# Eight more dummy matmuls in the head of an attention and expert-mixing kernel

## Chip, cores, metric

One core of one Trainium2 chip. The metric is the device time of one launch in microseconds (us). The profiler's span of an execution is 1.7 to 2.4 us shorter than its time; both are used below, and it is said which. Faster or slower needs 2%.

## The reference

Attention with decay (RetNet) over 8 batches, 8 heads, 576 positions and 64 values a head; its output goes through four experts, each two matmuls with a ReLU, weighted by normalised probabilities. Shortened:

```python
def _attn_ref(q, k, v):
    scores = scale * np.matmul(q, k.transpose(0, 1, 3, 2))
    # Dmat[h, i, j] = gamma[h] ** (i - j) for i >= j, else 0
    return np.matmul(scores * Dmat, v)

def _moe_ref(x, domain_probs, w1, w2):
    p = domain_probs / (domain_probs.sum(-1, keepdims=True) + 1e-09)
    for e in range(E):
        out += p[:, e:e + 1] * (np.maximum(x @ w1[e], 0.0) @ w2[e])
```

Here x has 4608 rows of 512 values, w1 is 4 x 512 x 1024 and w2 is 4 x 1024 x 512.

## The kernel before

Nearly the whole run is one stream of expert matmuls, in whose gaps the attention of batches 1 to 7 is done. Only batch 0 has nothing to hide in. Its first 512 positions are computed first, as fast as its loads allow, in four units of 256 positions and four heads each. A unit goes through: scaling of k (GpSimd) and q (VectorE) and a cast of v (GpSimd); transposes of q and k on TensorE (T); scores (S) and their mask on VectorE; states k'v (kv); outputs (O), and casts of these to the bf16 tile x on VectorE. Between them stand dummy matmuls with a zero operand, which nobody reads (shortened):

```python
def warm(n):
    warm_out = bank("mm", [128, 512], FP32, name="warm_out")   # one of three PSUM banks in turn
    for _ in range(n):
        nc.tensor.matmul(warm_out, lhsT=kbd[:, 0, :], rhs=kbd[...], start=True, stop=True)
# ... cut ...
a0 = AttP(0)
warm(8)
for n, eng in (("k", nc.gpsimd), ("q", nc.vector), ("v", nc.gpsimd)):
    a0.cast(n, *UNITS[0], eng)
head = [up_classical(0, 0, lead=3, pause=True)]      # the first expert matmuls
for x, (hf, u) in enumerate(UNITS):
    a0.T(hf, u)
    if x == 0:
        warm(4)
    else:
        a0.O(*UNITS[x - 1])
    if x < 3:
        a0.cast("k", *UNITS[x + 1], nc.gpsimd)
        a0.cast("q", *UNITS[x + 1], nc.vector)
        if x:
            load_w1(0, x - 1)
        a0.cast("v", *UNITS[x + 1], nc.gpsimd)
    a0.S(hf, u)
    if x == 0:
        warm(2)
    a0.kv(hf, u)
transposed_probs()
next(head[0])
a0.O(*UNITS[3])
```

The loads of batch 0 are issued at the very start on one queue, in the order k, q, v of unit 0, of unit 1, and so on.

## Time and profile before

| | before |
|---|---|
| time, median of 3 runs | 515.59 us (514.83 to 515.84) |
| span of the profiled execution | 514.5 us |
| TensorE busy | 504.1 us, 98% |
| TensorE's share of the chain that ended last | 92% |

In a timeline row the columns are start and duration in us, engine (PE is TensorE, DVE VectorE, ACT ScalarE, POOL GpSimd), source line, operation, output and inputs, shape, count, and in brackets the idle time ahead with what ended it. Ends of matmuls are modelled, so rows overlap a little. "The stream" below is the long run of first expert matmuls (line 525) that starts at 21.30 us in this trace.

### The profile page before, as it was taken

The page shows a single profiled execution, that of the slowest core. Times are in us where ns is not written, and L with a number is a line of the kernel's source. Part 1 is how long each engine was busy: PE and PEld are TensorE (multiplying, and loading weights), DVE is VectorE, ACT ScalarE, POOL GpSimd, SP SyncE. Part 2 cuts the span into 40 slices and gives each one's busy share as a digit, 9 for nine tenths or more (in the row PEclk, how much of TensorE's full clock was granted, in tenths as well). Part 3 has the DMA queues.
Part 4 walks back from the last instruction along what each step waited for, and adds up shares of the span by engine and source line. Part 5 has one row for each costly group of instructions (what it writes and reads, how often), then busy time and mean ns, then how long its engine had stood idle before and what let it go on. Part 6 is the DMA issues. An engine that isn't in the chain of part 4 may idle for free.

```text
span 514.5 us, 12795 instructions
## 1 busy us (share of the span) xinstructions
PE 504.1 (98%) x4923; PEld 405.7 (79%) x4934; DVE 374.4 (73%) x696; ACT 336.0 (65%) x693; POOL 251.1 (49%) x345
## 2 busy tenths in 40 slices
PE   8999999999999999999999999999999999999995
PEld 3644455688888888888888888888888888888884
DVE  5724479878777777768777877886778777667785
ACT  3462263677667766777767776777777767777663
POOL 6702275756644656466645664476457521321012
PEclk9999999999999999999999999999999999999998
DMA  9999997959797799969997999789987652565002
GB/s 239 187 207 201 208 196 184 165 146 186 120 172 194 115 177 161 182 142 183 133 223 140 162 153 212 159 144 154 173 195 122 94 83 83 83 86 80 1 2 82
DMA packets 160749, 76.27 MB, mean 148 GB/s; under 512 B 131724, under 2 KB 144524, under 8 KB 160688
## 3 DMA queue, kind: packets, MB, share of 16 engines
q1 hardware_dynamic: 141648, 44.79, 44.8%
q0 software_dynamic: 18752, 30.41, 38.2%
q8 instruction: 38, 0.62, 0.5%
q10 hardware_dynamic: 288, 0.26, 0.2%
q14 instruction: 23, 0.19, 0.1%
HBM read 45.16 MB, written 31.46 MB: 149 GB/s over the span
## 4 chain that ended last, share of the span: by engine, by line
PE 92%; DVE 5%; issue 1%; DMA 1%; ACT 0%; SPq 0%; DVEq 0%; ACTq 0%
PE upP L691 21%; PE downV L645 20%; PE downW L645 15%; PE upR L691 10%; PE ph L525 7%; PE po L564 6%; PE upQ L691 5%; PE s L328 2%; PE oc L379 1%; PE kvp L346 1%; PE oc L376 1%; DMA raw<-in_q_dram 1%; PE warm_out L164 1%; DVE qm L420 1%; DVE sT L333 0%
## 5 line engine op out<-in xcount | busy, mean ns | idle before, releaser
L691 PEld LDWEIGHTS <-wt 128*128 128x128 bf16 x992 | 94.9, 98 | 14.5 <-issue 1.4
L645 PEld LDWEIGHTS <-hT 128*128 128x128 bf16 x960 | 93.7, 98 | 12.0
L716 POOL TENSOR_SCALAR hT<-hT 128x512 bf16<-128x512 bf16 x62 | 38.1, 614 | 108.9 <-DVE hT L715 108.7
L645 PE MATMUL downV<-wt,hT 128*128 128x256 bf16 x480 | 81.8, 272 | 0.0
L691 PEld LDWEIGHTS <-wsum 128*128 128x128 bf16 x744 | 72.6, 98 | 9.1 <-issue 0.2
L707 DVE TENSOR_TENSOR upR<-upP,m 128x512 f32<-128x512 f32 x62 | 43.3, 699 | 48.6 <-ACT downW L651 39.9
L645 PEld LDWEIGHTS <-hsum 128*128 128x128 bf16 x720 | 70.0, 98 | 8.8 <-DVE hsum L617 0.3
L691 PE MATMUL upP<-xT,wt 128*128 128x256 bf16 x496 | 74.4, 272 | 0.7 <-DVE xT L595 0.5
L723 ACT ACTIVATE hT<-upP 128x512 bf16<-128x512 f32 x62 | 37.0, 597 | 52.0 <-PE upP L691 36.8
L514 POOL DMA_DIRECT2D out_dram<-acc x42 | 51.3, 1221 | 30.7 <-ACT acc L672 23.9
L674 DVE TENSOR_SCALAR acc<-downV,probs 128x512 f32<-128x512 f32 x56 | 42.0, 749 | 30.1 <-PE downV L645 29.7
L718 ACT ACTIVATE hT<-upR 128x512 bf16<-128x512 f32 x62 | 37.0, 597 | 31.3 <-PE upR L691 31.3
L709 ACT ACTIVATE hT<-upQ 128x512 bf16<-128x512 f32 x62 | 37.0, 597 | 15.9 <-PE upQ L691 15.9
L715 DVE TENSOR_TENSOR hT<-upP,m 128x512 bf16<-128x512 f32 x62 | 42.8, 690 | 5.8 <-PE upP L691 4.4
L672 ACT ACTIVATE acc<-downW,probs 128x512 f32<-128x512 f32 x56 | 38.6, 690 | 9.2 <-PE downW L645 9.2
L340 POOL TENSOR_SCALAR_AFFINE_SELECT sT<-sT 128x512 bf16<-128x512 bf16 x24 | 15.4, 643 | 57.4 <-ACT sT L339 48.0
L541 ACT ACTIVATE hT<-ph 128x512 bf16<-128x512 f32 x40 | 23.5, 597 | 29.8 <-PE ph L525 28.9
L697 ACT ACTIVATE upQ<-upP 128x512 f32<-128x512 f32 x62 | 37.0, 597 | 2.5 <-PE upP L691 2.3
L691 PE MATMUL upP<-tsum,wt 128*128 128x256 bf16 x248 | 37.2, 273 | 0.0
L691 PE MATMUL upR<-tsum,wsum 128*128 128x256 bf16 x248 | 37.2, 273 | 0.1
L691 PE MATMUL upP<-tsum,wsum 128*128 128x256 bf16 x248 | 37.2, 273 | 0.0
L691 PE MATMUL upR<-xT,wsum 128*128 128x256 bf16 x248 | 37.2, 273 | 0.0
(149 smaller groups left out, 1032.9 us busy)
## 6 DMA issues: line engine op xcount, KB each, us to landing
out_dram<-acc POOLq DMA_DIRECT2D x42, 512.0 KB, 6.5
out_dram<-acc SPq DMA_DIRECT2D x14, 512.0 KB, 4.1
wt<-in_moe_w_dram POOLq DMA_DIRECT2D x6, 1024.0 KB, 25.2
raw_k<-in_k_dram SPq DMA_DIRECT2D x24, 256.0 KB, 4.4
raw_q<-in_q_dram SPq DMA_DIRECT2D x24, 256.0 KB, 3.5
raw_v<-in_v_dram SPq DMA_DIRECT2D x24, 256.0 KB, 4.2
raw<-in_k_dram SPq DMA_DIRECT2D x8, 256.0 KB, 5.6
raw<-in_q_dram SPq DMA_DIRECT2D x8, 256.0 KB, 5.6
```

The lines of the kernel that those rows point to most:

```text
L514: i = nc.gpsimd.dma_start(out=out_rows[:, x, :], in_=acc[nt, j], accum_op=ADD)
L645: nc.tensor.matmul(o, lhsT=l[:, k, self.s * 128:(self.s + 1) * 128], rhs=r[:, k], start=(i == 1 and k == 0), stop=(k == NFC // 2 - 1), ski ...
L672: nc.scalar.activation(a, po, Copy, scale=pe)
L674: nc.vector.tensor_scalar_mul(a, po, pe)
L691: nc.tensor.matmul(ps[:, l], lhsT=wa(kc)[:, f:f + 128], rhs=xa(kc), start=(start and l == 0 and kc == 0), stop=(kc == 1), skip_group_check ...
L697: nc.scalar.activation(Q, P, Copy)
L707: nc.vector.tensor_tensor(R_, P, m5, op=ADD)
L709: nc.scalar.activation(hT[:, lo, t0], Q, Relu)
L715: nc.vector.tensor_tensor(h22, P, m5, op=ADD)
L716: nc.gpsimd.tensor_scalar(h22, h22, float("inf"), 0.0, op0=MIN, op1=MAX)
L718: nc.scalar.activation(hT[:, lo, t1], R_, Relu)
L723: nc.scalar.activation(hT[:, hi, t0], P, Relu)
```

## The change

Two more dummies fill the wait ahead of the first transposes, and two stand in the wait behind the states of units 0, 1 and 2. The intent is to keep TensorE busy so that it reaches its full rate earlier and stays there: in the trace of before, four transposes take 0.61 us at 5.70 and 0.39 us at 10.48.

```diff
     a0 = AttP(0)
-    warm(8)
+    warm(10)
     for n, eng in (("k", nc.gpsimd), ("q", nc.vector), ("v", nc.gpsimd)):
@@
         if x == 0:
             warm(2)
         a0.kv(hf, u)
+        if x < 3:
+            warm(2)
     transposed_probs()
```

## The prediction

"The gate" is a name for the change of TensorE's rate between the rows at 5.70 and 10.48 us: "open" is full rate, "shut" half rate. The marked cuts are statements about it that no trace on record showed: when full rate would come, what brings it or keeps it, and, in rival 2, that transposes might not help to bring it. The times under "What that buys" rested on a step, that full rate comes soon after the first transposes; it was the author's estimate. The 0.216 us of a dummy at full rate: the trace of before shows it for matmuls of 512 columns (24 of line 525 take 5.18 us from 48.68 on). The sum: 0.71 us won on VectorE, less 0.1, is 0.6; executions of the kernel before that reach full rate even later than its trace: the estimate of 0.1 more; so 0.7 us, and 515.6 - 0.7 = 514.9 us.

> **What bounds the kernel now.** I read the page first (busy shares, chain), then the TensorE timeline of the first 22 us, the waits from 20 us to the end, and the VectorE and ScalarE timelines of the same first 22 us. From the page:
>
> ```profile
> span 514.5 us, 12795 instructions
> PE 504.1 (98%) x4923; PEld 405.7 (79%) x4934; DVE 374.4 (73%) x696; ACT 336.0 (65%) x693; POOL 251.1 (49%) x345
> PE 92%; DVE 5%; issue 1%; DMA 1%; ACT 0%; SPq 0%; DVEq 0%; ACTq 0%
> ```
>
> TensorE carries 92% of the chain. The waits after 20 us show how little can still be taken away there; of all TensorE matmul waits (not weight loads) the listing has one line:
>
> ```profile
> PE upP L691 <- DVE xT L595: 0.5, 2, 0.3
> ```
>
> So from about 21 us on the kernel is a stream of matmuls, and a change in the head is worth exactly the shift of the moment at which that stream starts. The TensorE timeline of the head (start, duration, count, idle before):
>
> ```profile
> 1.26 3.60 PE L164 MATMUL warm_out<-kbd 128*128 128x512 bf16 x8 [1.26 <-DVE kbd L159]
> 5.70 0.61 PE L429 MATMUL pt<-ident,qm 128*128 128x128 bf16 x4 [0.85 <-DVE qm L420]
> ...
> 6.53 1.91 PE L164 MATMUL warm_out<-kbd 128*128 128x512 bf16 x4
> 8.38 0.64 PE L463 MATMUL s<-qkT 64*64 64x128 bf16 x16
> 8.95 1.03 PE L164 MATMUL warm_out<-kbd 128*128 128x512 bf16 x2
> 9.92 0.72 PE L447 MATMUL kvp<-vm,km 64*128 64x128 bf16 x8
> 10.48 0.39 PE L429 MATMUL pt<-ident,qm 128*128 128x128 bf16 x4
> 10.70 0.39 PE L429 MATMUL pt<-ident,km 128*128 128x128 bf16 x4
> 11.02 0.42 PE L481 MATMUL o<-sT,vm 64*64 64x128 bf16 x16
> ...
> 13.46 0.40 PE L429 MATMUL pt<-ident,qm 128*128 128x128 bf16 x4 [0.32 <-DVE qm L420]
> ...
> 16.48 0.40 PE L429 MATMUL pt<-ident,qm 128*128 128x128 bf16 x4 [0.20 <-DVE qm L420]
> ```
>
> Four transposes last 0.61 us at 5.70 and 0.39 us at 10.48: one tensor, one shape, two speeds. All 14 dummy matmuls have the long duration (609 to 634 ns); the states at 9.92 have the short one (216 to 230 ns). So TensorE runs at half speed until some moment between 9.4 us (start of the last dummy) and 9.92 us. The page's granted clock is 1.00 in this stretch, so that column does not show this gate. VectorE in the same stretch:
>
> ```profile
> 4.85 0.79 DVE L420 TENSOR_TENSOR qm<-raw,gq 128x512 bf16<-128x512 f32 x1 [1.54 <-DMA raw<-in_q_dram]
> ...
> 8.35 0.81 DVE L420 TENSOR_TENSOR qm<-raw,gq 128x512 bf16<-128x512 f32 x1 [1.15 <-DMA raw<-in_q_dram]
> 9.13 1.29 DVE L469 TENSOR_TENSOR sT<-s,tri 128x512 bf16<-128x512 f32 x2
> 11.13 0.42 DVE L433 COPY qkT<-pt 128x512 bf16<-128x512 bf16 x1 [0.71 <-PE pt L429]
> ```
>
> The second q scaling waits for its load until 8.35 us: no dummy matmul changes that. The masks follow until 10.42 us. Then VectorE idles 0.71 us for the transposes of unit 1, which TensorE has late because scores, dummies and states of unit 0 ran at half speed. After that VectorE works nearly without a hole until the attention of batch 0 is done. These 0.71 us are what can be won.
>
> [...]continuous work starts at 5.70 and full speed comes 3.7 to 4.2 us later. [...]The trace: (3.60 - 0.63)/7 = 0.424 us per dummy. Full-speed dummies are not in this trace[...].[...]
>
> **The change, part by part.** It removes nothing; it adds eight dummy matmuls with their weight loads, and three turns of the ring of three PSUM banks. As three is a whole round, every later bank is the same; the instruction order differs on TensorE by eight pairs and no real matmul changes its place.
>
> Part one, 8 to 10 dummies in front. They now start at 1.26 + 9 x 0.424 = 5.08 us for the last one, which ends near 5.08 + 0.63 = 5.71. The transposes could start at 5.70 anyway, when qm is written (4.85 + 0.79 = 5.64). So it costs 0.0 us, and fills the 0.85 us hole. TensorE is then busy without a hole from 1.26 us[...].
>
> What that buys: the four dummies after the first transposes end near 7.2 instead of 8.4; scores (needing both qkT copies, about 7.0) then 7.2 to 7.6, two dummies to 8.0, states to 8.6. The transposes of unit 1 start when their q is scaled, 8.35 + 0.81 = 9.16, so near 9.2 instead of 10.48, and end near 9.8. VectorE then goes from its masks (10.42) straight into the copy of the transposes: 0.71 us earlier. O of unit 0 starts with the masks' end, 10.45 instead of 11.02, and no longer holds up the casts.
>
> Part two, two dummies behind the states of units 0, 1, 2. At full speed each pair is 2 x 0.216 = 0.43 us. Unit 0: states end near 8.6, the transposes wait for 9.16, so the pair fits. Unit 1: the hole is 0.32 us, the pair overhangs by 0.11 us. Unit 2: hole 0.20 us, overhang 0.23 us. Behind units 1 and 2 the transposes' reader on VectorE is busy with masks (until 14.6 and 17.6 us in the trace, against transposes ending near 14.1 and 17.1), so 0.5 us of slack takes up both overhangs. I charge 0.1 us.[...]
>
> Sum: 0.71 won on VectorE, less 0.1, is 0.6 us, which passes to the matmul stream at about 21 us if nothing else ends last there. I checked the loads: the third unit's q lands at 5.43 + 5.6 = 11.0 us, and is now wanted at about 11.6; the first half of the first weight lands at 11.21 + 6.8 = 18.0 and is wanted near 19.4 instead of 20.07. [...]515.6 - 0.7 = 514.9 us.
>
> **Rivals.** (1) The dummies lie on the path. For it: they sit in TensorE's in-order stream, and TensorE is the bound. Against: all stand before 17 us, where VectorE and loads set the pace. If the three pairs were wholly exposed, 3 x 0.43 = 1.3 us, at half speed 2.6 us; with no gain 516.9 to 518.2. (2) The early gate brings nothing, since unit 1's q comes at 8.35 and the masks end at 10.42 whatever TensorE does. For it: both are true. Against: the hole of 0.71 us comes after them and is named as waiting for transposes.[...] (3) The shift is swallowed later, by loads that come at fixed times. For it: the transposes of batch 1 read casts that wait for loads; the closest ends at 70.20 + 1.04 = 71.24 for a transpose at 72.63. Against: 1.4 us of slack is more than 0.7. If swallowed, 515.3 to 515.6. (4) The kernel before opens late far more often than its profile shows, and the change cures it: 1.2 us or more, 514.2. Its three times span 1.0 us[...].
>
> **Range and chances.** Main case (60%) 514.5 to 515.2; nothing gained (20%) near 515.6; larger gain (13%) near 514.2; loss (7%) above 515.9. With 0.5 us of scatter between executions, 514.1 to 515.8 should hold it 8 times in 10. Two per cent is 10.3 us, and the whole stretch that the change can reach is 20 us, of which the loads alone fill most: within 2% 0.985, faster 0.01, slower 0.005.
>
> **What would show each step.** Ten dummies in one run from 1.26 to 5.7 and no hole before the first transposes: else part one costs. Dummies after the first transposes with a shorter duration than 609 ns, scores near 7.2 to 8.1: else the gate did not move. Transposes of unit 1 near 9.2 and VectorE's first copy of them near 10.4 without a hole of 0.71: else rival 2. The transposes of units 2 and 3 no later than 13.4 and 16.5: else rival 1. The matmul stream starting at 20.6 instead of 21.30, and the transposes of batch 1 at 66.0 instead of 66.70: if the first holds and the second does not, rival 3. I am wrong if the gate opens at an unchanged time, or if the head gets shorter and the end does not.

## The result

The changed kernel took 515.04 us (median of 4 runs, 514.71 to 515.26), the kernel before 515.67 us (4 runs, 514.83 to 515.84). The ratio is 0.9991 with a 95% interval of 0.9973 to 1.0008: the same by the 2% rule, and by the clock alone not even told from nothing. (One execution of the kernel before, of 580.49 us, with a span of 578.7 us and a mean granted clock of 0.852, was slow and is left out. A ratio is the mean time of one kernel's fast runs over that of the other's of the same rounds, so not quite the ratio of the medians. All runs used below were fast.)

The page of the changed kernel, its span and busy line:

```profile
span 513.3 us, 12823 instructions
PE 504.6 (98%) x4942; PEld 405.5 (79%) x4942; DVE 374.5 (73%) x696; ACT 336.2 (66%) x693; POOL 250.6 (49%) x345
```

The profiled span is 1.2 us shorter. TensorE in the head of the changed kernel, the rows that answer to those in the prediction:

```profile
1.26 4.45 PE L164 MATMUL warm_out<-kbd 128*128 128x512 bf16 x10 [1.26 <-DVE kbd L159]
5.66 0.42 PE L429 MATMUL pt<-ident,qm 128*128 128x128 bf16 x4
...
6.13 1.03 PE L164 MATMUL warm_out<-kbd 128*128 128x512 bf16 x4
7.09 0.42 PE L463 MATMUL s<-qkT 64*64 64x128 bf16 x16
...
7.98 0.72 PE L447 MATMUL kvp<-vm,km 64*128 64x128 bf16 x8
8.54 0.59 PE L164 MATMUL warm_out<-kbd 128*128 128x512 bf16 x2
8.97 0.40 PE L429 MATMUL pt<-ident,qm 128*128 128x128 bf16 x4
...
12.07 0.39 PE L429 MATMUL pt<-ident,qm 128*128 128x128 bf16 x4
...
15.09 0.39 PE L429 MATMUL pt<-ident,qm 128*128 128x128 bf16 x4
```

The ten dummies run up to the first transposes without a hole. Those take 0.42 us instead of 0.61, and the four dummies behind them 1.03 instead of 1.91: TensorE reached full rate before 5.7 us, not between 9.4 and 9.9. Each pair lasts 0.43 us to the start of the next row (8.54 to 8.97), as estimated. VectorE of the changed kernel:

```profile
8.12 0.80 DVE L420 TENSOR_TENSOR qm<-raw,gq 128x512 bf16<-128x512 f32 x1 [1.36 <-DMA raw<-in_q_dram]
8.84 1.27 DVE L469 TENSOR_TENSOR sT<-s,tri 128x512 bf16<-128x512 f32 x2
10.04 0.41 DVE L433 COPY qkT<-pt 128x512 bf16<-128x512 bf16 x1
...
11.26 0.68 DVE L420 TENSOR_TENSOR qm<-raw,gq 128x512 bf16<-128x512 f32 x1
```

The hole of 0.71 us ahead of the copy at 11.13 is gone: the copy follows the masks. The stream starts at 19.83 instead of 21.30, 1.47 us earlier. Going down VectorE's rows one can see where each part comes from:

| row on VectorE | before | changed | earlier by | what was added |
|---|---|---|---|---|
| second q scaling (waits for its load) | 8.35 | 8.12 | 0.23 | 0.23, the load |
| masks of unit 0 | 9.13 | 8.84 | 0.29 | 0.06 |
| copy of unit 1's transposes | 11.13 | 10.04 | 1.09 | 0.80, the hole |
| casts of unit 0's output | 11.48 | 10.58 | 0.90 | -0.19, now waiting, probably for O |
| third q scaling | 12.16 | 11.26 | 0.90 | 0 |
| masks of unit 1 | 13.33 | 11.86 | 1.47 | 0.57, a shorter q scaling |

After this row all are 1.47 us earlier. The last addition was not foreseen: the third q scaling takes 0.68 us and not 1.24. VectorE's scaling and GpSimd's cast in the kernel before, then the cast in the changed one:

```profile
12.16 1.24 DVE L420 TENSOR_TENSOR qm<-raw,gq 128x512 bf16<-128x512 f32 x1
...
12.21 0.63 POOL L422 CAST vm<-raw 128x512 bf16<-128x512 f32 x1
```

```profile
11.96 0.64 POOL L422 CAST vm<-raw 128x512 bf16<-128x512 f32 x1
```

In before, the scaling (12.16 to 13.40) has this cast inside it. In the changed kernel it ends (11.94) as the cast begins. The difference, 1.24 - 0.68 = 0.56 us, is near the length of the cast, 0.63 us. That the one comes from the other was a guess here; experiment 5 takes the cast away.

Not all of the 1.47 us arrived. The transposes of batch 1's third unit, before and changed:

```profile
72.63 0.39 PE L309 MATMUL ptc<-ident,qm 128*128 128x128 bf16 x4
```

```profile
71.61 0.40 PE L309 MATMUL ptc<-ident,qm 128*128 128x128 bf16 x4 [0.29 <-POOL qm L279]
```

There the lead shrinks to 1.02 us, as the scaled q from GpSimd, which waits for loads, was not ready. From there to the last products the lead is 1.0 to 1.1 us.

### The profile page after: what moved, and what is told of

It is laid out like the page before. It is cut to its first block, busy times and chain, and to the rows that moved or that the text cites. A ratio compares the mean times of both kernels' runs of the same rounds, so it can differ in the third digit from the quotient of the medians.

```text
span 513.3 us, 12823 instructions
## 1 busy us (share of the span) xinstructions
PE 504.6 (98%) x4942; PEld 405.5 (79%) x4942; DVE 374.5 (73%) x696; ACT 336.2 (66%) x693; POOL 250.6 (49%) x345
## 4 chain that ended last, share of the span: by engine, by line
PE 81%; DMA 10%; DVE 3%; SPq 3%; POOL 2%; issue 1%; ACT 0%; DVEq 0%; POOLq 0%; ACTq 0%
PE upP L691 21%; PE downV L645 20%; PE downW L645 15%; PE upR L691 10%; DMA raw<-in_q_dram 6%; PE upQ L691 5%; PE po L564 3%; DMA wt<-in_moe_w_dram 3%; PE s L328 2%; SPq L105 1%; PE ph L525 1%; PE oc L379 1%; PE kvp L346 1%; PE oc L376 1%; DMA raw<-in_v_dram 1%
## 5 line engine op out<-in xcount | busy, mean ns | idle before, releaser
L691 PE MATMUL upQ<-xT,wt 128*128 128x256 bf16 x248 | 37.2, 273 | 0.0
```

The lines of the kernel that those rows point to most:

```text
L691: nc.tensor.matmul(ps[:, l], lhsT=wa(kc)[:, f:f + 128], rhs=xa(kc), start=(start and l == 0 and kc == 0), stop=(kc == 1), skip_group_check ...
```

## The experiments

Twelve runs were made, three of them repeats of a kernel, each with a profile, in five timed rounds (four to six executions). All gave correct results. The first four shared one chip, the other eight another. My theory after the result: the filled hole in front brings TensorE from half to full rate earlier (before 5.7 us in the changed kernel, 9.4 to 9.9 in before), which removes VectorE's wait of 0.71 us for transposes; the pairs are mostly neutral. The rival: the pairs do it. A third reading: nothing but the scatter of loads. For all traces this is the table; "full rate from" is when TensorE's rows change from the long to the short duration (with "about", worked out from how many dummies of a row had the long spacing of 0.427 and how many the short of 0.216 us, or from a row of mixed length, so an estimate). The two later stretches at half rate are worked out from the granted clock in windows of half a microsecond.

| trace | full rate from | second q scaling starts | stream starts | difference | span |
|---|---|---|---|---|---|
| before, first | 9.4 to 9.9 | 8.35 | 21.30 | 12.95 | 514.5 |
| before, second | about 3.9; half rate again 10.7 to 14.15 | 8.75 | 21.22 | 12.47 | 514.1 |
| changed, first | before 5.7 | 8.12 | 19.83 | 11.71 | 513.3 |
| changed, second | about 4.7 | 8.70 | 20.42 | 11.72 | 513.3 |
| ten in front alone, first | about 6.1 | 8.33 | 20.05 | 11.72 | 512.9 |
| ten in front alone, second | about 4.3 | 7.99 | 19.70 | 11.71 | 512.6 |
| pairs alone | before 5.7 | 8.48 | 20.20 | 11.72 | 513.1 |
| transposes in front | about 5.8 | 8.20 | 19.88 | 11.68 | 513.1 |
| before, v cast of unit 2 on ScalarE | about 10.5 | 8.30 | 20.92 | 12.62 | 513.9 |
| pairs of six | about 7.2 | 8.45 | 21.65 | 13.20 | 514.7 |
| no dummies after the front | before 5.7; half rate again 8.7 to 15.55 | 8.28 | 20.84 | 12.56 | 514.1 |
| changed, a cast on ScalarE | about 6.3 | 8.03 | 19.58 | 11.55 | 512.3 |
| the same without pairs | about 7.2 | 8.36 | 19.91 | 11.55 | 512.4 |
| the same with pairs, q of unit 1 first | about 4.9 | 7.41 | 19.57 | 12.16 | 511.9 |

Three things are seen at once. Where full rate came by 6.1 us and stayed, and the code of VectorE is the kernel's own, the stream starts 11.68 to 11.72 us behind the second q scaling, in six traces of four kernels. Where it came late or was lost again, the difference is 12.5 to 13.0. And the second q scaling itself, which waits for a load, starts anywhere from 7.99 to 8.75 us with the same load order: a scatter as large as the gain. A fourth carries the theory: with ten matmuls in front full rate came by about 7.2 us in all nine traces; with eight it did so in two (3.9 and before 5.7) and in the other two only at 9.4 us or later.

### 1. The front alone

```diff
-        if x < 3:
-            warm(2)
```

(against the changed kernel)

> Ten dummies in front, no pairs behind the states. My theory ([...]the pairs mostly sit in waits): [...]first copy on VectorE straight behind the masks at about 10.0, matmul stream at 19.5 to 20.3 us, span within 0.2 us of the changed kernel, 515.0 us. Rival (the pairs do it[...]): no better than the kernel before, 515.6 us, stream at about 21.

Measured: 514.66 us, ratio to before 0.9983 (0.9967 to 0.9998); six spans from 512.6 to 513.6, mean 512.98, where ten fast spans of before in the same job have the mean 513.72. Stream at 20.05. The front part alone gives the whole gain, so the rival, that the pairs do it, falls.

### 2. The pairs alone

```diff
-    warm(10)
+    warm(8)
```

> Eight dummies in front as before, pairs behind the states. My theory: [...]the pair behind the first states is then still at half speed and on the path (0.85 us): stream at 21 to 22 us, 515.6 to 516.3 us. Rival (the pairs do it): stream at about 20, 515.0 us.

Measured: 516.25 us, ratio 1.0011 (0.9995 to 1.0027). By the clock the pairs alone bring nothing that can be told apart from zero; if anything they cost. But the trace was a surprise: full rate came before 5.7 us with the front of the kernel before (four transposes in 0.40 us at 5.63), stream at 20.20, span 513.1. The other five executions had spans of 514.2 to 515.3. So with the eight dummies full rate comes early in some executions (before 5.7 us here) and not in others (9.4 to 9.9 in the first trace of before). That the longer ones ran the pair behind the first states at half rate is my reading; they have no trace.

### 3. The kernel before, once more

No edit. The expectation names two alternatives, another moment of the change or the same one.

> The kernel before once more, word for word: a null for the timing and a second trace. [...]the gate opens elsewhere[...] than in the first trace (9.4 to 9.9) and the stream starts elsewhere than 21.30; ratio to before 0.999 to 1.001. [...]the same opening within 0.1 us.

Measured: 515.68 us, ratio 1.0007 (0.9979 to 1.0036); six spans from 512.5 to 517.5 us. In this trace TensorE changes its rate at other moments. Its rows:

```profile
1.26 3.19 PE L164 MATMUL warm_out<-kbd 128*128 128x512 bf16 x8 [1.26 <-DVE kbd L159]
5.60 0.40 PE L429 MATMUL pt<-ident,qm 128*128 128x128 bf16 x4 [1.15 <-DVE qm L420]
...
9.62 0.40 PE L429 MATMUL pt<-ident,qm 128*128 128x128 bf16 x4 [1.00 <-DVE qm L420]
...
10.82 0.64 PE L481 MATMUL o<-sT,vm 64*64 64x128 bf16 x14 [0.35 <-DVE sT L469]
...
13.22 0.63 PE L429 MATMUL pt<-ident,qm 128*128 128x128 bf16 x4
...
14.21 0.42 PE L481 MATMUL o<-sT,vm 64*64 64x128 bf16 x16
```

The eight dummies take 3.19 us and not 3.60, so the last of them ran at full rate, which came at about 3.9 us. TensorE had full rate at 9.62 (0.40 us for four transposes), half rate at 10.82 (14 matmuls of line 481 in 0.64 us, against 0.41 at 17.60) and at 13.22 (0.63 us for four transposes), and full rate again at 14.21 (16 of line 481 in 0.42 us). The granted clock, which was 1.00 through the first half rate of every trace, does show this second one, with 0.50 from 11.0 to 14.0. Windows of half a microsecond of the same trace (columns: window, its length, busy time and count of PE, weight loads, DVE, ACT and POOL, then granted clock, DMA share, GB/s):

```profile
10.50:11.00 0.50, 0.18 (x9) 0.18 (x12) 0.50 (x2) 0.21 (x1) 0.39 (x1) 0.73 1.15 289
...
14.00:14.50 0.50, 0.50 (x19) 0.27 (x17) 0.22 (x2) 0.48 (x2) 0.50 (x2) 0.85 0.73 127
```

A clock of 0.73 means 0.23 us at full rate and 0.27 at half, so the change lies at 10.73; by the same working it changes back at 14.15, after 3.42 us. From 3.9 to 10.73 are 6.83 us, twice as much. To compare stretches I count back from the loss in this length; that is an estimate, and no trace shows that anything is decided at the end of such a stretch. The one from 7.31 to 10.73 held the hole of 1.00 us and the first 0.26 us of that of 0.35, and at its end full rate was lost; TensorE was busy for 2.15 of its 3.42 us. The one before it, from 3.90 to 7.31, held the hole of 1.15 us (busy for 2.26 of 3.41 us), and full rate stayed. A single hole of 1.15 us was thus not enough to lose it here. This was new to me, and it gives the pairs a possible purpose: they fill just that first hole of 1.00 us. The granted clock of a whole execution now tells how long it ran at half rate after full rate had first come: with 0.50 at half rate, a mean of 0.995 over 514 us is 0.005 x 514 / 0.5 = 5 us, of which up to about 3 us can be the idle end (in the first trace of before the clock is 0.93 from 510 to 512 us and 0.50 from 512 on). The execution with the span of 517.5 us had 0.987, about 13 us. Where the expectations above took for granted that full rate comes late in the kernel before, this trace refutes them, since in part of the executions it comes early.

### 4. The changed kernel, once more

No edit.

> The changed kernel once more, on the same chip with the parts: 515.0 us, ratio 0.9985 to 0.9995.[...] Transposes of the third unit of batch 1 at 71.5 to 71.7 us, held by the q scaling on GpSimd, whatever the head did.

Measured: 514.90 us, ratio 0.9984 (0.9967 to 1.0001); spans 512.6 to 513.5, mean 513.07. Full rate came at about 4.7 and stayed, across a hole of 0.64 us ahead of unit 1's transposes (four of them in 0.40 us behind it): there the pair had run, and the load was late (8.70). Together with a later hole of 0.35 us that makes 0.99 us from 8.16 to 11.58, of which TensorE was busy for 2.43 us (a stretch placed by counting on from 4.75 in the length of experiment 3, so an estimate). The stream is 11.72 us behind the second q scaling as in the first trace. The transposes of batch 1's third unit came at 71.75 with no wait, 51.33 us behind the stream as in before (72.63 - 21.30), so the 0.45 us lost there in the first trace were a matter of that execution, and "held by the q scaling on GpSimd, whatever the head did" was wrong.

### 5. The v cast of unit 2 on ScalarE, in the kernel before

```diff
+            elif eng is nc.scalar:
+                eng.activation(o, i, Copy)
@@
-            a0.cast("v", *UNITS[x + 1], nc.gpsimd)
+            a0.cast("v", *UNITS[x + 1], nc.scalar if x == 1 else nc.gpsimd)
```

> The kernel before, but the v cast of unit 2 moved from GpSimd to ScalarE. Theory: the q scaling of unit 2 on VectorE, 1.24 us in the trace of before and 0.68 us in that of the changed kernel, is stretched by this v cast, which runs at the same time in before and not in the changed one. Then it takes 0.68 to 0.75 us here, and the stream starts 0.4 to 0.6 us earlier than in before for the same gate opening, near 20.7. Rival (its length comes from something else, such as the half speed of TensorE or the q load): it stays at 1.2 us.

Measured: 515.88 us, ratio 1.0004 (0.9992 to 1.0017). The third q scaling and the copy ahead of it, on VectorE:

```profile
11.30 0.42 DVE L435 COPY qkT<-pt 128x512 bf16<-128x512 bf16 x1 [1.00 <-PE pt L431]
...
12.35 0.68 DVE L420 TENSOR_TENSOR qm<-raw,gq 128x512 bf16<-128x512 f32 x1
```

The scaling takes 0.68 us, though full rate came late (about 10.5 us) and it starts later than in before: with the cast off GpSimd the 0.56 us are gone (it ran on ScalarE, from 12.20 to 12.83, beside the scaling). In the trace this is worth 0.33 us at the stream (12.62 against 12.95 behind the q scaling), as the hole ahead of the copy is 1.00 here and not 0.71. By the clock nothing is left. In the second trace of before the third scaling took 0.68 us as well (a cast on GpSimd began at 12.60, near its end) and the fourth 1.01 (a cast from 15.17 to 15.79, across its start at 15.34), so which scaling is stretched changes from one execution to the next; taking one cast away does not move the mean by more than this run can tell.

### 6. Transposes as dummies in front

```diff
-    warm(10)
+    warm_t = bank("mm", [128, 2, 256], BF16, name="warm_t")
+    for _ in range(36):
+        nc.tensor.transpose(warm_t[:, 0, :128], kbd[:, 0, :], ident)
```

> The changed kernel with 36 dummy transposes of 128 columns in place of the ten dummy matmuls in front: about the same time on TensorE[...], so no hole either. If transposes count as busy for the gate: [...]result as the changed kernel, 515.0 us. If they do not: [...]the second group of dummies at half speed (1.9 us for four), result as before or later, 515.6 to 516.3 us.

Measured: 515.64 us, ratio 0.9998 (0.9986 to 1.0011), five spans from 513.1 to 514.3, mean 513.50 (before 513.78). TensorE's first rows:

```profile
1.79 4.00 PE L730 MATMUL warm_t<-ident,kbd 128*128 128x128 bf16 x36 [1.79 <-POOL ident masks.py:199]
5.62 0.52 PE L429 MATMUL pt<-ident,qm 128*128 128x128 bf16 x4
...
6.20 1.03 PE L164 MATMUL warm_out<-kbd 128*128 128x512 bf16 x4
```

The 36 take 4.00 us. The four transposes at 5.62 take 0.52 us, between 0.61 and 0.40: full rate came inside this row, and up to then TensorE had run nothing but transposes (made with `nc.tensor.transpose`; the trace lists them as MATMUL). So in this execution 4.0 us of transposes and nothing else were enough. The mean time is that of before all the same, which this theory did not expect; the dummies start 0.53 us later (they need a constant from GpSimd), and the executions without a trace may have reached full rate late. That stays open.

### 7. Six dummies in place of each pair

```diff
         if x < 3:
-            warm(2)
+            warm(6)
```

> The changed kernel with six dummies in place of two behind the states of units 0, 1, 2: 4 x 0.216 = 0.86 us more on TensorE each time, 2.6 us in all. Theory (pairs lie in slack: VectorE's masks end 0.4 to 0.6 us after the transposes): exposed is only the part beyond the slack, about 0.3 to 0.5 us per unit, 1.0 to 1.5 us at the stream, of which the wait at 71.6 us takes back up to 0.45: 515.6 to 516.1 us. Rival (every dummy is paid in full): 2.6 us, 517.6 us.

Measured: 516.52 us, ratio 1.0014 (1.0000 to 1.0028), mean span 514.30. Six dummies take 1.29 us (9.18 to 10.47), 0.215 each. The 2.6 us of additional dummies cost 1.48 us at the stream (13.20 against 11.72 behind the q scaling). VectorE shows how they come onto the path:

```profile
11.12 0.42 DVE L433 COPY qkT<-pt 128x512 bf16<-128x512 bf16 x1 [0.69 <-PE pt L429]
...
18.13 0.42 DVE L433 COPY qkT<-pt 128x512 bf16<-128x512 bf16 x1 [0.45 <-PE pt L429]
```

The holes for transposes are back; and the third q scaling (12.14, 1.32 us) has GpSimd's cast (12.28, 0.63 us) inside it again. So dummies behind the states lie beside other work only up to the slack of the masks, as the prediction had it: a pair fits, six do not.

### 8. One of the two output casts of each unit on ScalarE

```diff
             for c in range(2):
-                put_x(nc.vector, slice(2 * u, 2 * u + 2), self.b * S + 256 * hf + c * C, os[c])
+                put_x(nc.vector if c else nc.scalar, slice(2 * u, 2 * u + 2), self.b * S + 256 * hf + c * C, os[c])
```

(in the changed kernel, dummies as there)

> The changed kernel with one of the two casts of each unit's output moved from VectorE to ScalarE, which makes the head shorter by 2 or 3 times 0.3 us: stream at about 19.0 to 19.3 us. Theory (loads that come at fixed times hold the transposes of batch 1's third unit at about 71.6 us): hardly any of it at the end, stream earlier by 0.5 or more but those transposes still at 71.5 to 71.7, 514.9 to 515.1 us. Rival (the end follows the stream): 514.4 us.

Measured: 514.04 us (513.50 to 514.26), ratio 0.9969 (0.9957 to 0.9982). Every run is below the fastest run of before in the same job (514.89). The remaining cast takes 0.42 us where two took 0.76, but the stream starts 11.55 us behind the q scaling, only 0.17 less, since that cast now waits for O (0.37 to 1.02 us). Batch 1's transposes came 51.33 us behind the stream without a wait, so my theory of loads at fixed times falls and the rival (the end follows the stream) stands. That the mean gained more over the changed kernel than the head shows (span 512.26, against 513.07 on another chip, where before had nearly the same mean span) I can't fully explain: the interval from stream to last products is 0.16 us shorter in its trace, and 0.46 and 0.55 us shorter in those of experiments 11 and 12. So part of this cast's gain lies behind the head, for a cause that stays open.

### 9. No dummies after the front

```diff
-        if x == 0:
-            warm(4)
-        else:
+        if x:
             a0.O(*UNITS[x - 1])
@@
-        if x == 0:
-            warm(2)
         a0.kv(hf, u)
-        if x < 3:
-            warm(2)
```

> The ten dummies in front kept, every later dummy taken out (the four, the two, the pairs), so TensorE idles about 0.5 us ahead of the first scores and about 1.5 to 2 us ahead of the second unit's transposes. New theory, from the second trace of the kernel before (gate open from about 4, shut from about 11 to 14 us, after a window with holes of 1.0 and 0.35 us)[...]. [...]stream 12.0 us or more behind the start of the second q scaling; spans as the kernel before, 513.5 to 514.5 us. Rival[...]: stays open, stream 11.7 us behind the second q scaling as in the changed kernel.

Measured: 516.46 us, ratio 1.0018 (1.0005 to 1.0032), spans 514.1 to 514.7. TensorE:

```profile
5.70 0.40 PE L429 MATMUL pt<-ident,qm 128*128 128x128 bf16 x4
...
6.83 0.42 PE L463 MATMUL s<-qkT 64*64 64x128 bf16 x16 [0.52 <-ACT qkT L436]
...
9.12 0.61 PE L429 MATMUL pt<-ident,qm 128*128 128x128 bf16 x4 [1.21 <-DVE qm L420]
...
16.02 0.40 PE L429 MATMUL pt<-ident,qm 128*128 128x128 bf16 x4
```

The theory here was that holes like those of experiment 3 (1.00 and 0.35 us) end full rate, the rival that they do not. TensorE had full rate at 5.70 and 6.83 (four transposes in 0.40, 16 scores in 0.42 us), half rate at 9.12 (0.61 us), and full rate again only at 16.02; by the granted clock, at half rate from 8.72 to 15.55, which is 6.83 us, twice the 3.42 of experiment 3. The longest hole was 1.21 us, of which 0.82 had passed when full rate was lost; in the 3.41 us up to then (5.31 to 8.72, the length again by the estimate of experiment 3) TensorE was busy for 1.96 us. All five executions have a mean clock of 0.991 to 0.995, so all of them lost the rate. So full rate was lost here, as in the second trace of before, without a hole of more than 1.21 us; and it came back late though TensorE was busy again: 6.08 of the 6.10 us from 9.1 to 15.2, all at a granted clock of 0.50. With all dummies but the front's taken out, the head loses all that the front won and more (mean span 514.48 us, before 513.78): the four and the two that were in the kernel already are needed to keep what the front wins.

### 10. The front alone, once more

The edit of experiment 1.

> Ten in front and no pairs, once more, for what the pairs are worth. If the pairs matter (they fill the hole ahead of the second unit's transposes[...]): some executions 0.5 to 1 us longer than the changed kernel's, spans 512.6 to 514.3, mean 0.2 to 0.4 us above it. If they do not: spans 512.6 to 513.6 as in the first such run, mean within 0.2 us of the changed kernel.

Measured: 515.37 us, ratio 0.9995 (0.9981 to 1.0008), but spans 512.6 to 513.4, mean 512.96, as in the first such run. By the spans the pairs are worth nothing beside the front; by the times this run is between before and changed. In its trace full rate came at about 4.3 and stayed; the second q came early (7.99), so the hole of 1.00 us that came before the loss in the second trace of before did not arise.

### 11. The cast on ScalarE without the pairs

Experiment 8 with the edit of experiment 1.

> The changed kernel with one output cast of each unit on ScalarE, and without the pairs. The run with the pairs gave 514.04 us. If the pairs matter: 514.2 to 514.6 us with a wider scatter. If they do not: 513.9 to 514.1 us.

Measured: 514.39 us (4 runs, 514.06 to 515.51), ratio 0.9981 (0.9967 to 0.9995); spans 512.4, 512.4, 513.0 and 513.8, against 511.8 to 512.5 with the pairs. That is what the theory of useful pairs expected, but four runs against five, and the opposite of experiment 10. What the pairs are worth beside the front is thus not settled. The clocks say that they are not needed against losing full rate: of 40 executions with ten matmuls in front and the older inner dummies, 15 of them without pairs, none has a mean clock below 0.997, while 3 of 26 fast executions of before have 0.987 to 0.995.

### 12. The q of unit 1 loaded ahead of its k

```diff
-            for n, src in SRC:
+            for n, src in (SRC[1], SRC[0], SRC[2]) if x == 1 else SRC:
```

(on top of experiment 8)

> The changed kernel with one output cast of each unit on ScalarE, and the q of unit 1 loaded before its k. In all traces with the gate open the stream starts 11.7 us behind the second q scaling (11.55 with the cast on ScalarE), and that scaling waits for its load. Theory (this load sets the head): second q scaling at 7.2 to 7.6 instead of 8.0 to 8.7, then the k of unit 1 is late (transposed copies at about 9.7), so 0.3 to 0.5 us at the stream: 513.5 to 513.7 us. Rival (the k scaling on GpSimd, now later, takes its place in full): 514.0 us or more.

Measured: 513.85 us (513.63 to 513.97), ratio 0.9966 (0.9954 to 0.9979), spans 511.9 to 512.3. VectorE:

```profile
7.41 0.69 DVE L420 TENSOR_TENSOR qm<-raw,gq 128x512 bf16<-128x512 f32 x1 [0.69 <-DMA raw<-in_q_dram]
...
9.96 0.42 DVE L433 COPY qkT<-pt 128x512 bf16<-128x512 bf16 x1 [0.66 <-PE pt L429]
```

The q scaling starts 0.62 us earlier than in experiment 8, and the copy of the transposes at the same time (9.96 against 9.95): a hole of 0.66 us appears, in which TensorE waited for the k from GpSimd. The rival was right: one wait took the place of the other. The mean, 513.83 against 513.98 us, is not told apart. Experiments 8 and 12 are the two fastest kernels and beat both given ones.

## Why the prediction was right, point by point

- **What bounds.** Right. In the eleven traces without experiment 8's cast, the last group of products starts 486.75 to 486.88 us behind the stream in eight (both of before and the second of the changed kernel among them), and 487.14 to 487.24 in three: a shift of the stream is passed on, less at most 0.5 us.
- **Front part costs nothing and fills the hole.** Right: the dummies end at 5.71, the transposes start at 5.66 (before 5.70), with no idle time.
- **When full rate comes.** Right that it comes earlier: at about 4.3 to 7.2 us in the nine traces with ten matmuls in front. The forecast's own bounds for both kernels are cut, as no trace had shown what they rested on. For the kernel before they held in one trace (9.4 to 9.9) and were wrong in the other (about 3.9), when TensorE had been busy for only 2.6 us since its first matmul, with a second stretch of half rate at 10.7. What decides when full rate comes was not shown: experiments 2 and 5 start with the same eight dummies (3.60 us) and holes of 0.78 and 0.74 us, and it came before 5.7 in one and at about 10.5 in the other. The sentence that the granted clock does not show this change was too wide as well: it shows both later stretches at half rate (0.50) but is 1.00 until full rate first comes. The kernel before does not always lose the 0.71 us in the way that its first trace shows.
- **The hole on VectorE, 0.71 us.** Right in place and size: 0.80 with the short gap between masks and copy.
- **The pairs, 0.1 us.** Right that the masks hide them, and the charge of 0.1 us was not needed. In the first trace of the changed kernel units 2 and 3 are transposed 0.13 us behind the end of their q scaling (12.07 against 11.94), and the stream starts 11.71 and 11.72 us behind the second q scaling with the pairs as without them (experiments 1 and 10). Six in place of two are not hidden.
- **Sum of 0.6 us at the stream.** Mis-sized for this pair of traces: 1.47 us, of which 0.23 is a load that came earlier. The missing term, 0.57 us, is the third q scaling, 0.68 us and not 1.24, with GpSimd's cast no longer inside it.
- **Rival 3, a gain swallowed by loads.** It happened in the first trace of the changed kernel (0.45 us at the transposes of batch 1's third unit) and not in the second, and in none of the other twelve traces, so the slack of 1.4 us was judged rightly for all traces but one.
- **The time.** 514.9 predicted, 515.04 measured, 514.90 in the repetition. It is partly luck that the two misses cancel: the head gains more than I worked out against the first trace, but that trace was one of the slower executions of before (516.28 us timed), whose spans run from 512.4 to 514.9 with one of 517.5.

## What to carry to other kernels

When a wait for data at the start of a kernel leaves TensorE idle, try to fill it with dummy matmuls. Here ten in front brought full rate by 4.3 to 7.2 us in all nine traces, where with eight it came at 9.4 us or later in two of four, and they cost nothing, as the fill ended about when the data were ready (first transposes at 5.66, before at 5.70). Beyond the slack dummies are paid: six in place of each pair cost 1.48 us of their 2.6. Later holes matter, too: here full rate was lost after stretches of 3.4 us in which TensorE was busy for 2.0 and 2.2 us, and kept after stretches with 2.3 and 2.4 (placed by the estimate of experiment 3). And for a change of this size take at least two traces of each kernel: one trace of each gave 1.2 us, of which the runs showed 0.6 to 0.8 on average.
